# Last pass of a decode backward kernel: later use of the weight slabs in the background products, and an earlier start of the next group's dO product

## The chip, the cores and the metric

The kernel runs on one core of one Trainium2 chip. The metric is the device time of one execution in microseconds (us), taken as the median over several executions. Smaller is better.

## The reference

The program is forward and backward of four small layers applied to one token (batch 1, sequence 1, model width 1024): attention over a cache, a dense layer with squared ReLU, the same attention again, the same dense layer again. The attention has 32 query heads in four groups of eight; each group shares one key and one value cache of 65536 rows of 128 bf16 numbers (16 MB each). Weights are shared between the two uses.

```
x = x + A(layernorm(x))      # A: q = x wq; softmax(q k^T / sqrt(128)) v; times wo
x = x + B(layernorm(x))      # B: relu(x w1 + b1)^2 w2 + b2
x = x + A(layernorm(x))
x = x + B(layernorm(x))
out, vjp = jax.vjp(f, x, k_cache, v_cache, wq, wo, w1, b1, w2, b2)
return out, vjp(grad_out)    # the output and nine gradients
```

The large results are the gradients of the two caches (64 MB each), which are sums over both attention layers.

## The kernel before

The work is one token, so almost all of it is moving the caches through on-chip memory. Four passes go over them: pass 1 and pass 2 are the two attention forwards, pass 3 is the backward of the second attention, and pass 4 is the backward of the first attention, which also writes the gradients of both caches. Between the passes stand short dense stages for the feed-forward layers.

**Blocks and items.** A cache of one group is read in blocks of 32 x 128 rows, 1 MB each. An item is a quarter of a block (eight 128x128 tiles). A group has 64 items and pass 4 has 256 items, in the order `ITEMS[3]`, groups 3, 2, 1, 0. `pipeline` runs over the items; in round i it calls the stage functions with their lags: `vT` (TensorE transposes eight V tiles at L1249, and the result is copied to `kt`), `vS` two items later (scores at L1282, and at the end of a block the product X at L1290), `dV8` (gradient of V) three items later, and `k8` (dq at L1329 and the gradient of K) seven items later. The gradient blocks are built by `outer16` (matmuls at L1303, copies to the arena, one store of 1 MB by the POOL queue at L1309). After the stages of a round `bg.step(i)` advances the background work by at most one step.

**The arena.** All large buffers are granules of 1 MB in one tile called `arena`: 12 free ones and 8 that hold the softmax weights of both layers (one per layer and group) until pass 4 is done with a group. `Slot` takes a granule: loads of cache blocks (L331, by the SP queue), weight slabs (L425, also by SP) and store buffers all come from the same supply. A weight slab takes the granule that has been free longest. A granule that was stored from may be loaded again only when its store has landed.

**The background products.** Two of them use weights in pass 4. `g_dO` multiplies one group's share of `wo` with the gradient dx1 and gives dO, which a group needs before its first item (`bg.need(g)` in `vT` would run the rest of it at once). `g_dn` does the same with `wq` once a group's dq is complete, at round 70 for the first group. Both go through `g_rowdots`. It takes eight rows from two slabs of 1 MB (four rows each), first builds a broadcast vector `vbc` in `g_bcast_vec` (four steps), and then issues one multiplication on VectorE per row (L553, `mv_t`), whose sum ScalarE takes at L544. A slab is requested when its first row is asked for; the first four rows come from the first slab, and before row 4 the generator yields `"wait"` five times (`WAIT_STEPS`), one round each.

`Background` has a queue `urgent`, worked strictly first in, first out, a queue `normal` (the gradients of the weights, worked only in rounds in which the urgent work waits or is absent), and a list `later` of products that join `urgent` at a given round. `by_group` fills `later`: in pass 4 the dO of the second, third and fourth group join at rounds 32, 96 and 160.

**Who sets the order.** Passes 1 to 3 run inside `tc.manual_schedule`, so TensorE, VectorE and ScalarE execute in the written order. Pass 4 does not: there a planner at build time orders each engine's instructions. Among instructions that it holds to be ready it takes the one written first, and an instruction written later may go ahead of earlier ones while those wait. Each engine and each DMA queue then executes in that fixed order, with semaphore waits.

Of the kernel before, what the change touches and what calls it, by code (L numbers as in the profile page):

```python
# [20 lines left out]
def kernel(  # L21
# [46 lines left out]
    WAIT_STEPS = 5  # L68
# [13 lines left out]
    PS = {}  # L82
# [5 lines left out]
    def ps_tr(shape=None, dtype=BF):  # L88
        return PS["pool"].tile(shape or [P, 8, P], dtype, name="ps_tr", tag="tr", bufs=2 if PS["pass4"] else 3)
# [4 lines left out]
    def ps_gg():  # L94
        return PS["pool"].tile([P, 1024], F32, name="ps_gg", tag="gg", bufs=2)
# [4 lines left out]
    def ps_mv(shape, dtype=F32):  # L100
        if PS["pass4"]:
            return ps_tr(shape, dtype)
        return PS["pool"].tile(shape, dtype, name="ps_mv", tag="mv", bufs=1)
# [30 lines left out]
    def add_load(act=0.0, dve=0.0, pe=0.0):  # L134
        load["act"] += act
        load["dve"] += dve
        load["pe"] += pe
# [379 lines left out]
    def g_bcast_vec(vcol, nj):  # L517
        pt = ps_mv([nj, P], F32)
        nc.tensor.transpose(pt[:, :], vcol, ident_f[:, :])
        yield  # L520
        rows = tmp.tile([32, P], BF, name="bc_rows")
        nc.vector.tensor_copy(out=rows[0:nj, :], in_=pt[:, :])
        vbc = mvs.tile([P, nj * P], BF, name="vbc", tag="vbc", bufs=1)
        yield
        for j0 in range(0, nj, 4):
            pg = ps_gg() if PS["pass4"] else ps_tr([P, 512], F32)
            for jj in range(4):
                nc.tensor.matmul(pg[:, jj * P:(jj + 1) * P], lhsT=ident_b[0:nj, j0 + jj:j0 + jj + 1].to_broadcast([nj, P]),
                                 rhs=rows[0:nj, :], start=True, stop=True)
            nc.scalar.copy(out=vbc[:, j0 * P:(j0 + 4) * P], in_=pg[:, 0:512])  # L530
            add_load(act=0.6)
            yield
        return vbc

    def g_rowdots(slab_it, nk, vcol, nj, finish, name):
        n = nj * P
        y = vec.tile([P, nk], F32, name=name)
        nc.gpsimd.memset(y[:], 0.0)
        vbc = None
        due = None  # L540

        def total(t, kc):
            def f():
                nc.scalar.activation(out=t[:, :], in_=t[:, :], func=ACTF.Copy, accum_out=y[:, kc:kc + 1])  # L544
            return f
        for kc, slab in slab_it:
            if vbc is None:
                vbc = yield from g_bcast_vec(vcol, nj)
            elif kc % 4 == 0:
                for _ in range(WAIT_STEPS):  # L550
                    yield "wait"
            t = mvs.tile([P, n], BF, name="mv_t", tag="mv_t", bufs=2)
            nc.vector.tensor_tensor(out=t[:, :], in0=slab, in1=vbc[:, :], op=ALU.mult)  # L553
            add_load(dve=0.1 + n * 0.00054, act=0.42 + n * 0.00083)
            if due is not None:
                due()
            due = total(t, kc)
            yield
        due()
        yield  # L560
        r = finish(y[:, :])
        if r is not None:
            yield from r
        yield
# [167 lines left out]
    class Background:  # L732
# [35 lines left out]
        def by_group(self, p, gen):  # L768

            order = list(dict.fromkeys(g for g, _ in ITEMS[p]))  # L770
            n = len(ITEMS[p]) // G
            for k, g in enumerate(order[1:]):
                self.later.append((k * n + n // 2 if PS["pass4"] else k * n + n // 4, gen(g), g))

        def drain(self):
            while self.later:
# [115 lines left out]
    def g_dO(L, dx, g):  # L892
        yield from g_rowdots(wo_slabs(g)[0], R, dx[:], DC, dO_finish(L, g), "%s_dO%d" % (L["name"], g))
# [10 lines left out]
    def g_dn(L, dn, g, first):  # L904
        yield from g_rowdots(wq_slabs(g)[0], DC, L["dqT"][:, gsl(g)], R, dn_finish(dn, first), "%s_dn%d" % (L["name"], g))
# [770 lines left out]
```

## Time and profile before

| what | value |
|---|---|
| median of 8 runs | 2013.25 us |
| lowest and highest run | 2009.19 and 2017.61 us |
| profiled execution, its own time | 2017.61 us |
| its span in the trace | 2015.8 us |
| pass 4 in the trace, first and last X at L1290 | 1221.5 to 1980.8 us |
| read from and written to memory | 625 MB and 166 MB |
| mean rate over the span | 392 GB/s |
| PE, DVE, ACT, POOL busy | 81%, 58%, 52%, 7% of the span |

The profiled execution is the slowest of the eight, 4.4 us above the median. Its own time is 1.8 us more than its span. The first X and the last X lie 63 blocks apart, so a block of pass 4 takes 12.05 us on average and an item 3.0 us.

A row of the page's groups names the line, the engine, the operation and the tiles written and read, then the busy time and the mean duration, and after the bar the engine's idle time just before these instructions with what ended most of it. In the views by time the columns are start, duration, engine, line and operation, and in square brackets the idle time before.

### The profile page before, as it was taken

To read this page: it belongs to the slowest core of one execution; us is meant where nothing else is said; L and a number is where in the kernel's file an instruction comes from. 1 tells how busy PE (TensorE), PEld (TensorE's weight loads), DVE (VectorE), ACT (ScalarE), POOL (GpSimd) and SP (SyncE) were. 2 spreads that over 40 slices of the span, in tenths; PEclk is the share of its full clock that TensorE was granted. 3 is DMA by queue.
4 is the path that set the end of the run, shared out by engine and by line. 5 is a ranking of instruction groups with operands and counts; after the bars stand their busy time and mean duration, and the time that the engine had idled before them with its cause. 6 is when DMAs were issued, how large, how long until landed. Compare 5 with 4: busy or idle time off the path is not lost. (4 is left out here: it accounts for less than half of the span.)

```text
span 2015.8 us, 67001 instructions
## 1 busy us (share of the span) xinstructions
PE 1622.8 (81%) x30210; PEld 1317.9 (65%) x30210; DVE 1175.0 (58%) x2358; ACT 1043.9 (52%) x1613; POOL 144.4 (7%) x332
## 2 busy tenths in 40 slices
PE   6877788688877787878777888788788898698986
PEld 6877777687777786767677785455455455355554
DVE  5645455355545544535454466587668587578775
ACT  3444344253443353426353355586667587567665
POOL 0000000000000000000000001111111121111211
PEclk9989899698999997998998998799779699789888
DMA  9999999999999998999999986999999899899996
GB/s 389 421 419 420 419 423 402 392 399 419 420 418 421 419 400 313 365 419 420 420 417 413 391 304 262 356 407 424 420 417 421 343 422 422 355 423 425 423 369 242
DMA packets 110845, 794.97 MB, mean 394 GB/s; under 512 B 9424, under 2 KB 9438, under 8 KB 49374
## 3 DMA queue, kind: packets, MB, share of 16 engines
q1 hardware_dynamic: 86510, 624.99, 76.1%
q0 software_dynamic: 24048, 165.70, 19.9%
q8 instruction: 236, 3.87, 0.8%
q14 instruction: 51, 0.42, 0.1%
HBM read 624.96 MB, written 165.69 MB: 392 GB/s over the span
## 5 line engine op out<-in xcount | busy, mean ns | idle before, releaser
L153 DVE COPY kt<-ps_tr 128x1024 bf16<-128x1024 bf16 x724 | 497.4, 688 | 473.4 <-PE ps_tr L936 256.3
L150 ACT CAST arena<-ps_gg 128x1024 bf16<-128x1024 f32 x452 | 441.1, 1010 | 221.9 <-PE ps_gg L1303 173.5
L936 PE MATMUL ps_tr<-ident_b,arena 128*128 128x128 bf16 x3840 | 311.1, 226 | 62.1 <-DMA arena<-in_A_k_cache_dram 46.6
L936 PEld LDWEIGHTS <-arena 128*128 128x128 bf16 x3840 | 235.2, 101 | 69.1 <-DMA arena<-in_A_k_cache_dram 49.5
L153 DVE CAST arena<-ps_gg 128x1024 bf16<-128x1024 f32 (+1 forms) x191 | 228.8, 1198 | 82.6 <-PE ps_gg L1303 45.4
L150 ACT COPY kt<-ps_tr 128x1024 bf16<-128x1024 bf16 x164 | 171.2, 1049 | 184.6 <-PE ps_tr L1128 125.5
L1303 PE MATMUL ps_gg<-GG,xt 64*128 64x512 bf16 x1024 | 218.4, 424 | 49.4 <-DVE arena L153 28.4
L1038 PE MATMUL ps_acc<-arena 128*128 128x64 bf16 (+4 forms) x4096 | 205.8, 196 | 43.8 <-DMA arena<-in_A_v_cache_dram 25.8
L1249 PE MATMUL ps_tr<-ident_b,arena 128*128 128x128 bf16 x1824 | 179.6, 237 | 28.9 <-DMA arena<-in_A_v_cache_dram 28.1
L954 PE MATMUL ps_sc<-L_qpad,kt 128*128 128x64 bf16 (+7 forms) x3584 | 183.8, 194 | 17.5 <-issue 9.9
L1128 PE MATMUL ps_tr<-ident_b,arena 128*128 128x128 bf16 x1920 | 155.7, 227 | 51.6 <-DMA arena<-in_A_v_cache_dram 50.9
L1019 ACT ACTIVATE arena<-S_sb,L_negm 128x128 bf16<-128x128 f32 x256 | 165.6, 1003 | 56.7 <-DVE L_negm L1004 56.7
L1038 PEld LDWEIGHTS <-arena 128*128 128x128 bf16 x4096 | 159.9, 100 | 46.9 <-DMA arena<-in_A_v_cache_dram 29.8
L1249 PEld LDWEIGHTS <-arena 128*128 128x128 bf16 x1824 | 120.7, 105 | 86.7 <-issue 54.4
L954 PEld LDWEIGHTS <-kt 128*128 128x128 bf16 x3584 | 153.5, 100 | 22.2 <-issue 12.3
L1128 PEld LDWEIGHTS <-arena 128*128 128x128 bf16 x1920 | 117.7, 101 | 56.2 <-DMA arena<-in_A_v_cache_dram 53.8
L1329 PE MATMUL ps_acc<-X,arena 128*128 128x64 bf16 (+3 forms) x2048 | 120.4, 199 | 21.0 <-DMA arena<-in_A_k_cache_dram 21.0
L1019 ACT ACTIVATION_READ_ACCUMULATOR arena<-S_sb,L_negm 128x1 f32 x256 | 128.2, 501 | 0.0
L1329 PEld LDWEIGHTS <-arena 128*128 128x128 bf16 x2048 | 87.7, 102 | 56.1 <-issue 33.1
L1303 PEld LDWEIGHTS <-xt 64*128 64x128 bf16 x1024 | 61.1, 94 | 91.2 <-issue 54.2
L1282 PEld LDWEIGHTS <-kt 128*128 128x128 bf16 x1824 | 87.1, 104 | 50.1 <-issue 48.7
L1282 PE MATMUL ps_sc<-DOB,kt 128*128 128x64 bf16 (+3 forms) x1824 | 119.6, 202 | 0.0
(269 smaller groups left out, 2152.1 us busy)
## 6 DMA issues: line engine op xcount, KB each, us to landing
arena<-in_A_k_cache_dram SPq DMA_DIRECT2D x86, 2048.0 KB, 21.8
arena<-in_A_v_cache_dram SPq DMA_DIRECT2D x83, 2048.0 KB, 21.2
out_dram<-arena POOLq DMA_DIRECT2D x151, 1024.0 KB, 11.6
arena<-in_A_v_cache_dram SPq DMA_DIRECT2D x76, 1024.0 KB, 14.9
arena<-in_A_k_cache_dram SPq DMA_DIRECT2D x76, 1024.0 KB, 12.6
arena<-in_B_w_dram SPq DMA_DIRECT2D x32, 896.0 KB, 6.7
arena<-in_A_wq_dram SPq DMA_DIRECT2D x22, 1024.0 KB, 14.5
arena<-in_A_wo_dram SPq DMA_DIRECT2D x18, 1024.0 KB, 18.6
```

The lines of the kernel that those rows point to most:

```text
L150: nc.scalar.copy(out=out, in_=in_)
L153: nc.vector.tensor_copy(out=out, in_=in_)
L936: nc.tensor.transpose(pt[:, i, :], kb8[:, i, :], ident_b[:, :])
L954: nc.tensor.matmul(state["ps_s"][:, s:s + w, :].rearrange("p a b -> p (a b)"), lhsT=kt[:, i, :], rhs=L["qpad"][:, g, 0:w, :].rearrange("p ...
L1019: nc.scalar.activation(out=E(p, g, c0, SU)[:, :, h], in_=S[:, h, :], func=ACTF.Exp, bias=L["negm"][:, g, su, h:h + 1], scale=SCALE, accum_ ...
L1038: nc.tensor.matmul(ps_o[:, 0:w, :], lhsT=vb8[:, i, :], rhs=E(p, g, c, w), start=(c % SU == 0), stop=(c % SU == SU - 1), skip_group_check=True)
L1128: nc.tensor.transpose(pt[:, i, :], vb8[:, i, :], ident_b[:, :])
L1249: nc.tensor.transpose(pt[:, i, :], vb8[:, i, :], ident_b[:, :])
L1282: nc.tensor.matmul(state["ps_dp"][:, s:s + w, :].rearrange("p a b -> p (a b)"), lhsT=vt[:, i, :], rhs=DOB[:, g, 0:w, :].rearrange("p a b - ...
L1303: nc.tensor.matmul(pg[:, 512 * h:512 * h + 512], lhsT=xt[64 * h:64 * h + 64, j1 // 8 + m, :], rhs=gg[64 * h:64 * h + 64, :, :].rearrange(" ...
L1329: nc.tensor.matmul(ps_dq[:, 0:w, :].rearrange("p a b -> p (a b)"), lhsT=kb8[:, i, :], rhs=X[:, s:s + w, :].rearrange("p a b -> p (a b)"), ...
```

## The change

In `g_rowdots` the number of waiting steps is eight in pass 4 and five elsewhere. They stand before row 4 as before. New are waits after `g_bcast_vec`, before the first row: `steps - WAIT_STEPS + 1`, which is four in pass 4, and one in pass 3, which uses the same function. In `by_group` the second group's dO of pass 4 joins the urgent queue at round 16 instead of 32, the third group's at 72 instead of 96, and the fourth group's at 136 instead of 160.

```diff
@@ g_rowdots
         due = None
+        steps = 8 if PS["pass4"] else WAIT_STEPS
...
         for kc, slab in slab_it:
             if vbc is None:
                 vbc = yield from g_bcast_vec(vcol, nj)
+                for _ in range(steps - WAIT_STEPS + 1):
+                    yield "wait"
             elif kc % 4 == 0:
-                for _ in range(WAIT_STEPS):
+                for _ in range(steps):
                     yield "wait"
@@ by_group
             for k, g in enumerate(order[1:]):
-                self.later.append((k * n + n // 2 if PS["pass4"] else k * n + n // 4, gen(g), g))
+                self.later.append((k * n + 8 if PS["pass4"] and k else k * n + n // 4, gen(g), g))
```

Lines of the kernel named here and below are those before the change.

## The prediction

> **What bounds the kernel now.** I read the windows of 50 us over pass 4 first, then the waits of the dip, then the engine and queue timelines at it.
>
> ```profile
> core 0: us, PE busy (x) PEld busy (x) DVE busy (x) ACT busy (x) POOL busy (x), PEclk, DMA share, GB/s
> 1200.00:1250.00 50.00, 37.31 (x603) 26.88 (x604) 34.33 (x87) 26.33 (x31) 7.40 (x15) 0.90 0.69 264
> 1250.00:1300.00 50.00, 40.84 (x472) 24.50 (x471) 30.16 (x46) 28.14 (x31) 8.87 (x17) 0.76 0.92 345
> 1300.00:1350.00 50.00, 41.07 (x487) 25.36 (x487) 36.06 (x60) 38.14 (x51) 7.39 (x14) 0.86 1.00 402
> ...
> 1700.00:1750.00 50.00, 30.53 (x394) 19.66 (x392) 29.64 (x47) 28.61 (x39) 6.39 (x12) 0.80 0.90 361
> 1750.00:1800.00 50.00, 45.51 (x608) 28.38 (x604) 39.56 (x69) 35.87 (x39) 11.18 (x21) 0.97 1.01 416
> ```
>
> The last two columns carry it: from 1300 us on the 16 DMA engines are full, except in a few dips. The bound of pass 4 is the transfers, and a stall costs what it takes from them. The first 100 us are not full: there granules are missing. The dip at 1700 has one cause:
>
> ```profile
> DVE mv_t L553 <- DMA arena<-in_A_wo_dram: 16.3, 1, 16.3
> ```
>
> ```profile
> 1712.32 1.27 DVE L153 COPY kt<-ps_tr 128x1024 bf16<-128x1024 bf16 x2
> 1729.90 0.69 DVE L553 TENSOR_TENSOR mv_t<-arena,vbc 128x1024 bf16<-128x1024 bf16 x1 [16.30 <-DMA arena<-in_A_wo_dram]
> ```
>
> ```profile
> 1703.42 0.33 SPq L331 DMA_DIRECT2D arena<-in_A_v_cache_dram  x1
> 1707.43 3.63 SPq L331 DMA_DIRECT2D arena<-in_A_k_cache_dram  x2
> 1711.17 0.44 SPq L425 DMA_DIRECT2D arena<-in_A_wo_dram  x1
> ```
>
> VectorE stands for one slab (fourth group's dO, row 4), and every copy from PSUM behind it stands too. The slab was issued at 1711.17 and landed 18.6 us later; VectorE arrived 2.4 us after the issue. Of the 12 slabs in pass 4 used this way it is the only one waited for. Why was it issued late? In the built program its granule (a softmax plane) has long been free, but SP works in order, and the K load ahead waits for a store:
>
> ```profile
> SPq L331 <- DMA out_dram<-arena: 539.9, 94, 14.5
> SPq L425 <- DMA out_dram<-arena: 76.3, 13, 9.4
> ```
>
> That is how SP lives in this pass: stores land (median 11.7 us), then it issues.
>
> **What the Trainium skill says.** "Perfetto Trace Analysis", section "Sequencer Loop": an engine's instructions are queued and each waits for its semaphores. The trace agrees: the copies behind the row stood 16.3 us. "DMA: Bandwidth & Descriptors", section "Issuing engines are not separate DMA queues": transfers of all issuers share the same engines and interleave. It agrees: the loads of SP take 76.1% and the stores of POOL 19.9% of the same 16 engines. So a slab competes with both. The same page, section "Measured", gives 6.15 us for 1 MB alone; here slabs of pass 4 landed after 7.5 to 30.3 us, median 14.3, and I use these.
>
> **The change part by part.** No arithmetic and no byte is added or removed: 96 rows, the same loads, the same stores. What moves is order. I compared the built programs' order on each engine, placing each instruction by the item whose work stands before it, and each load by what holds it or its predecessors on SP.
>
> (a) Waits. Per product, four before row 0 and three more before row 4; six products, 42 rounds in pass 4. They cost no engine time: normal background work takes the rounds. g_dn grows from 19 to 26 rounds, g_dO from 21 to 28. Will a group be kept waiting? The second pair runs from 70 to 95 and 96 to 123, before the need at 128; the third ends at 187, before 192. Cost 0. If they overran, the remaining rows would come at once, some 3 us.
>
> (b) The joining round. The queue is first in, first out, and g_dn joins at 70. So the dO that joins at 72 begins at 96, as before; the last at 160, as before. Only the second group's dO really moves, from 32 to 16. Cost of the rest 0.
>
> (c) Is the slab used eight items after its request? No: the planner pulls it forward. The stalled row was written at item 173.6 and stands after the copy of item 169.0; in the changed program it is written at 180.7 and stands after 174. The store that holds SP ahead of it moves too, from the one of item 162.6 to 166.6. Distance 6.4 items before, 7.4 after: one item gained, at about 2.5 us unstalled. **The wait does not go, it shrinks to about 13 us** (bounds 8 and 16). A saving in the end time is smaller: the dip took 10% of 50 us from the DMA engines, 5.0 us for 16.3 us of stall. So -1 us (bounds 0 and -3).
>
> (d) The second group's dO, at 16. Its second slab (row 4) now stands on SP behind a K load that waits for the scores of item 29, and the row stands on VectorE after the copy of item 29.8. Distance 0.7 items; before, the same slab had 7 to 8. So VectorE arrives 2 to 3 us after the issue, and loads land there in 7.5 to 11.1 us (K, V and slab loads of 1240 to 1320). **A new wait of 5 to 9 us**, with all copies behind it. DMA share there is 0.92, so the cover is thinner than at 1700: end time between a third of it and all, +2 to +9, taken +5.
>
> (e) Its first slab takes a granule that a K load had, when only 12 circulate. The K load for item 19 moves from behind the scores of item 13 to behind a store, and seven loads between items 19 and 40 have only 5 to 6.5 items from release to use (a store counted as five items), against three before. K and V waits of 1240 to 1320 are 17 us now. I take +2 us (bounds 0 and +8). On the other side, 1 MB leaves the full stretch at 1311 for a less full one, 1 MB at 421 GB/s: -1.5 us (bounds -2.5 and 0).
>
> (f) Third group's dO: its first slab gets 5.6 items, 17 us at 3.0 us, against a landing of 14 to 18.6. +0.5 us (0 to +3).
>
> (g) Pass 3: one wait in each of six products; no row waits there for a slab. SP moves a slab by one or two places. 0 (bounds -1 and +2).
>
> POOL's stores keep their number and nearly their order; some move past a neighbour, priced in the bounds of (e). Sum: -1 + 5 + 2 - 1.5 + 0.5 = +5. The profiled execution took 2017.61 us for a span of 2015.8, the slowest run shown; against it the changed kernel would take 2022.6, against the median of 2013.25 it is **2018 us**. Its own range, the bounds not all at one end: 2014 to 2026.
>
> **The rivals.**
>
> *Faster: the wait goes.* If the transfers ahead of the slab are lighter at 174 than they were, the row finds it landed, and (d) hides in the slack of the unfilled start. For it: landings range from 7.5 to 30.3 us, and the wait decides at a landing of about 5 us after issue, or at 6 items more of distance. Against it: SP's order shows 1 more item, and the three loads just ahead are still there. Gain: 5 us by DMA share, up to 12 if later blocks don't give it back. After the stall the trace gives back part already: the four blocks behind it took about 10 us against a mean of 12. So 2001 to 2008, say 2006.
>
> *No change.* The transfers bound the pass and a ring of granules absorbs what VectorE does: stalls only move. For it: share 1.00 to 1.02 in most windows. 2010 to 2016, about 2013.
>
> *Much slower: the start breaks.* With two slab granules out of 12 between items 13 and 40, each K load behind the SP queue comes late, and each late one delays the store that the next waits for. It decides when three or more of the seven tight loads each stall 4 to 8 us; with (d), 2026 to 2038.
>
> *The change doesn't do what it says* is in the forecast: (b) and (c).
>
> **How the numbers follow.** A difference under 0.2% (4 us) cannot be told from none. Forecast 45% (slower by more 36, same 9); start breaks 12% (slower); no change 21% (same 18, faster 2, slower 1); faster rival 22% (faster 20, same 2). Together faster 0.22, same 0.29, slower 0.49. The range reaches from inside the faster case to inside the broken start, 2004 to 2034.
>
> **What would show it.** Right: a wait of mv_t for in_A_wo in two places, one near item 30 (about 1285 us) and one near item 174 (about 1745), together 16 to 25 us; DMA share under 0.95 in a window at both; dO of the third group still beginning near item 96. Wrong: no wait of mv_t over 3 us (faster rival), or none near item 30 and the time unmoved (no change), or K and V waits of 1240 to 1320 at twice the 17 us (broken start).

## The result, and the profile after

The changed kernel takes **2024.63 us** (median of 11 runs, 2020.39 to 2031.16), the kernel before 2011.45 us beside it (median of 32). The ratio is 1.0062, with an interval of [1.0051, 1.0073]. The forecast was slower, by 5 us; it was slower by 12.5 us by the ratio (0.0062 of 2012; 13.2 us between the two medians). The profiled execution took 2023.42 us for a span of 2021.6 us. That is only 5.8 us more than the span of before, whose profiled execution was the slowest of those first shown. So the two traces show where the change acts, and the sizes must come from the runs.

In the lines below line numbers are higher than before from line 541 on, by 1 at L545 and by 3 from L556 on: `mv_t` is L556, X is L1293. `xin` (L1256 before, L1259 now) is a copy on POOL of the softmax weights of the next block.

The windows of 50 us over pass 4 first, with the same columns as those of before:

```profile
core 0: us, PE busy (x) PEld busy (x) DVE busy (x) ACT busy (x) POOL busy (x), PEclk, DMA share, GB/s
1200.00:1250.00 50.00, 36.03 (x606) 25.89 (x602) 34.56 (x84) 26.43 (x30) 7.12 (x14) 0.95 0.69 261
1250.00:1300.00 50.00, 39.26 (x459) 23.90 (x457) 32.23 (x44) 31.27 (x39) 7.82 (x16) 0.78 0.96 376
...
1500.00:1550.00 50.00, 34.20 (x421) 22.08 (x421) 31.52 (x57) 29.44 (x41) 6.52 (x12) 0.78 0.83 322
...
1700.00:1750.00 50.00, 30.96 (x309) 19.00 (x308) 21.81 (x34) 21.87 (x27) 5.24 (x10) 0.63 1.01 404
```

The window where the forecast put a new cost, 1250 to 1300, is fuller than before (0.96 against 0.92). The dip is at 1500 to 1550, where before had 1.01. Before had a dip of its own one window later, 0.90 at 1550 to 1600, which is 1.01 now; taken together, the two windows moved 1.15 MB less than before (745 against 768 GB/s in sum), which is about 3 us of transfers. At 1700 to 1750 the DMA engines are now full, but the compute engines still stand, with TensorE at 309 matmuls against 394. VectorE waited for weight slabs in pass 4 as follows (engine, tile and line, what ended the wait, total us, times, longest):

```profile
DVE X L1293 <- DMA arena<-in_A_wo_dram: 30.1, 2, 19.5
DVE mv_t L556 <- DMA arena<-in_A_wo_dram: 1.7, 1, 1.7
```

This is the odd line of the case. `mv_t` reads the slabs of `wo` and hardly waits. **X waits for them, 30.1 us in two places, and X reads no weight**: it multiplies scores with softmax weights. VectorE's timeline at the first and at the second:

```profile
1491.50 0.69 DVE L153 COPY kt<-ps_tr 128x1024 bf16<-128x1024 bf16 x1 [0.17 <-PE ps_tr L1252]
1511.67 0.69 DVE L1293 TENSOR_TENSOR X<-ps_sc,arena 128x512 bf16<-128x512 f32 x1 [19.48 <-DMA arena<-in_A_wo_dram]
```

```profile
1733.16 1.21 DVE L153 CAST arena<-ps_gg 128x1024 bf16<-128x1024 f32 x1
1744.97 0.69 DVE L1293 TENSOR_TENSOR X<-ps_sc,arena 128x512 bf16<-128x512 f32 x1 [10.59 <-DMA arena<-in_A_wo_dram]
```

And the loads on SP, from two stretches of its timeline, and `xin` on POOL ahead of the second slab:

```profile
1478.21 7.32 SPq L331 DMA_DIRECT2D arena<-in_A_v_cache_dram  x2
1485.62 0.65 SPq L331 DMA_DIRECT2D arena<-in_A_k_cache_dram  x1
1486.38 0.89 SPq L425 DMA_DIRECT2D arena<-in_A_wo_dram  x1
...
1728.37 0.56 SPq L425 DMA_DIRECT2D arena<-in_A_wo_dram  x1
```

```profile
1727.72 0.62 POOL L1259 COPY xin<-arena 128x512 bf16<-128x512 bf16 x1
```

The first slab was issued at 1486.38 and landed 25.2 us later, the second at 1728.37 and landed after 16.5 us. Both times VectorE was free for X about 6 us after the issue (1492.19 and 1734.37) and X stood until the landing. The second is the slab for which `mv_t` stood 16.3 us before the change. It went out 0.03 us after this `xin` had ended (1728.34).

What stood behind the first of them, in the timelines of TensorE and of POOL:

```profile
1512.42 0.61 PE L1265 MATMUL ps_tr<-ident_b,X 128*128 128x128 bf16 x4 [19.65 <-DVE X L1293]
```

```profile
1514.71 0.30 POOL L1232 CAST CC<-cf 128x128 bf16<-128x128 f32 x1 [22.23 <-PE ps_tr L1234]
```

TensorE's transposes of X and POOL's queue, which also issues the stores, waited as long. POOL issued no store between 1491.94 and 1518.36 us, and SP no load between 1502.87 and 1522.59. The transfers ran down only after the stall, as windows of 10 us show:

```profile
1500.00:1510.00 10.00, 0.00 (x0) 0.00 (x0) 0.00 (x0) 0.00 (x0) 0.00 (x0) 0.50 1.02 416
1510.00:1520.00 10.00, 7.58 (x66) 5.14 (x66) 4.46 (x8) 2.91 (x4) 2.10 (x4) 0.50 0.63 260
1520.00:1530.00 10.00, 8.85 (x117) 5.47 (x116) 8.53 (x15) 8.47 (x13) 1.15 (x2) 0.92 0.74 288
```

While every engine stood, loads and stores issued earlier kept the DMA engines full; then 6.3 us of their time were lost in 20 us. At the second stall SP issued two more loads (1740.41 and 1743.62), and the share fell only to 0.91 in the 10 us behind it.

**Why X waits.** X and `xin` take the softmax weights of both layers through one view, `E2(g)`: granule 12+g for one layer and 16+g for the other. In the built programs the semaphores are set as if such an access touched everything from 12+g to 16+g. A group that is done frees its two softmax granules, and a slab takes the oldest free granule. If it is one that lies between, it is bound on both sides to instructions that don't touch it. (An item number in the table says behind which item's work the instruction is written: X of item 165 belongs to the block of items 160 to 163.)

| slab, built program | granule | its load waits for | and then who waits for it |
|---|---|---|---|
| before: fourth dO's second, asked for in round 168 | 14 | X of item 165, xin of 167 | `mv_t`, one place ahead of X on VectorE, and xin of 171 |
| after: third dO's first, round 96 | 15 | X of item 93, xin of 95 | X of item 97, xin of 99 |
| after: fourth dO's second, round 172 | 14 | X of item 169, xin of 171 | X of item 173, xin of 175 |

So such a slab can't go out before the X or xin just ahead, and the next X can't run before it has landed. Whether the row is used five or eight items after the request doesn't matter: the X in between waits in any case. Before had one such slab, after has two, because other holding times and other rounds make another granule the oldest in round 96. I call this the **false operand**.

### The profile page after: what moved, and what is told of

It is laid out like the page before. It is cut to its first block, busy times and chain, and to the rows that moved or that the text cites. A ratio compares the mean times of both kernels' runs of the same rounds, so it can differ in the third digit from the quotient of the medians.

```text
span 2021.6 us, 67004 instructions
## 1 busy us (share of the span) xinstructions
PE 1617.3 (80%) x30210; PEld 1320.4 (65%) x30210; DVE 1173.5 (58%) x2361; ACT 1042.2 (52%) x1610; POOL 143.4 (7%) x332
## 5 line engine op out<-in xcount | busy, mean ns | idle before, releaser
L150 ACT CAST arena<-ps_gg 128x1024 bf16<-128x1024 f32 (+1 forms) x455 | 442.9, 1012 | 248.3 <-PE ps_gg L1306 193.7
L153 DVE CAST arena<-ps_gg 128x1024 bf16<-128x1024 f32 (+1 forms) x188 | 224.5, 1194 | 86.2 <-PE ps_gg L1306 40.9
L1306 PE MATMUL ps_gg<-GG,xt 64*128 64x512 bf16 x1024 | 214.1, 416 | 39.3 <-ACT arena L150 19.6
L1252 PE MATMUL ps_tr<-ident_b,arena 128*128 128x128 bf16 x1824 | 176.6, 235 | 30.3 <-DMA arena<-in_A_v_cache_dram 29.0
L957 PE MATMUL ps_sc<-L_qpad,kt 128*128 128x64 bf16 (+7 forms) x3584 | 183.8, 194 | 20.1 <-issue 13.2
L957 PEld LDWEIGHTS <-kt 128*128 128x128 bf16 x3584 | 153.5, 100 | 26.7 <-issue 16.9
L1176 PE MATMUL ps_acc<-dsT,arena 128*128 128x64 bf16 (+7 forms) x2048 | 105.5, 197 | 14.4 <-DMA arena<-in_A_k_cache_dram 11.6
L1285 PE MATMUL ps_sc<-DOB,kt 128*128 128x64 bf16 (+3 forms) x1824 | 114.5, 201 | 0.0
## 6 DMA issues: line engine op xcount, KB each, us to landing
arena<-in_A_k_cache_dram SPq DMA_DIRECT2D x76, 1024.0 KB, 12.5
```

Of the source, the lines that this page charges most:

```text
L150: nc.scalar.copy(out=out, in_=in_)
L153: nc.vector.tensor_copy(out=out, in_=in_)
L957: nc.tensor.matmul(state["ps_s"][:, s:s + w, :].rearrange("p a b -> p (a b)"), lhsT=kt[:, i, :], rhs=L["qpad"][:, g, 0:w, :].rearrange("p ...
L1176: nc.tensor.matmul(ps_dq[:, 0:w, :].rearrange("p a b -> p (a b)"), lhsT=kb8[:, i, :], rhs=dsT[:, s:s + w, :].rearrange("p a b -> p (a b)") ...
L1252: nc.tensor.transpose(pt[:, i, :], vb8[:, i, :], ident_b[:, :])
L1285: nc.tensor.matmul(state["ps_dp"][:, s:s + w, :].rearrange("p a b -> p (a b)"), lhsT=vt[:, i, :], rhs=DOB[:, g, 0:w, :].rearrange("p a b - ...
```

## The experiments

There are two ways to take the false operand away without touching a wait or a round. All ratios are against the kernel before, with 95% intervals.

**1. Slabs kept out of the softmax granules** (`after_low`: the changed kernel; `before_low`: the kernel before).

```diff
-        by_age = sorted((t, i) for i, t in FREE.items())
+        by_age = sorted((t, i) for i, t in FREE.items() if not low or i < NSLOT)
...
-                sl = Slot(name)
+                sl = Slot(name, low=PS["pass4"])
```

> The changed kernel, except that in pass 4 a weight slab takes only granules of the ring's first twelve, never a freed softmax plane. Theory of the false operand: X (the block product on VectorE) waited 30.1 us for in_A_wo although it reads no weight, because it reads the softmax weights of both layers through one access pattern over granules 12+g to 16+g, and a slab put between them is taken for its operand. Then here X waits less than 3 us for in_A_wo; the dip of 1500 to 1550 (DMA share 0.83, so 8.5 us of transfers lost) goes; time 8 to 13 us under the changed kernel: 0 to +5 us against the kernel before. Rival, held granules: the longer wait holds slabs' granules longer and K and V loads come late; then the X wait may go but the time stays at +10 to +13 us, or worse, since slabs now come out of the same twelve granules (+15 to +20). Rival, the early dO: the second group's dO at item 16 costs at the start; then +8 or more stays too, with X times behind by that much from block 10 on.

Measured: 2012.57 us, 0.9999 [0.9987, 1.0011]. X waits no more for `in_A_wo`; `mv_t` does for 3.7 us, near 1288 us. The windows at the two places:

```profile
1500.00:1550.00 50.00, 42.70 (x557) 27.15 (x556) 40.02 (x73) 39.30 (x52) 8.47 (x15) 0.93 1.00 406
...
1700.00:1750.00 50.00, 33.91 (x366) 20.79 (x364) 27.45 (x44) 26.95 (x34) 6.10 (x11) 0.73 0.96 368
```

The dip at 1500 is gone (share 1.00 against 0.83, 557 matmuls against 421). At 1700 TensorE does more than in the changed kernel (366 against 309), though less than in the one before, and the share is 0.96. With its slabs kept low the changed kernel is level with the kernel before: 0.0063 of the time goes.

> The kernel before with slabs of pass 4 kept to the first twelve granules. It has one slab between the planes that X reads (fourth group's dO, row 4), and mv_t stands 16.3 us for it just ahead of an X that would stand for it too. False operand: the slab's place alone doesn't move mv_t, which reads it in truth, so mv_t may still wait for it, 5 to 16 us, and the time is within -5 to +2 us of before. Held granules: fewer granules for K and V, +3 to +10 us.

Measured: 2007.33 us, 0.9970 [0.9960, 0.9981]. No row waits for a slab at all, so the expectation that `mv_t`'s wait might stay was wrong, and the gain, 6.0 us, is just past the 5 us that were expected at most. Experiment 2 shows that this wait too came from the false operand.

**2. The reads split by layer** (`after_split`, `before_split`): the granules stay as they are.

```diff
-                nc.gpsimd.tensor_copy(out=split2(xin[:, :, :]), in_=E2(g, c8, J))
+                for l in range(2):
+                    nc.gpsimd.tensor_copy(out=split2(xin[:, :, :])[:, :, l, :], in_=E(l, g, c8, J))
...
-                nc.vector.tensor_tensor(out=split2(X[:, :, :]), in0=split2(ps_dp[:, :, :]), in1=E2(g, c0, J), op=ALU.mult)
+                for l in range(2):
+                    nc.vector.tensor_tensor(out=split2(X[:, :, :])[:, :, l, :], in0=split2(ps_dp[:, :, :])[:, :, l, :],
+                                            in1=E(l, g, c0, J), op=ALU.mult)
```

> The changed kernel with the granules as they are, but the two reads of the softmax weights (VectorE's X product and GpSimd's xin copy) are each split into one instruction per layer, so that none spans the granules between. This adds 64 instructions on VectorE and 64 on GpSimd, X of 128x256 in place of 128x512; VectorE is busy 0.73 of the time, so some 0.2 us more for each pair is at most 13 us of busy time, most of it beside other work. False operand: no wait of X for in_A_wo, time 5 to 13 us under the changed kernel (0 to +8 against before). Held granules or early dO: the X wait goes and the time stays at +10 to +16.

Measured: 2011.28 us, 0.9993 [0.9982, 1.0003]; no wait of X for a slab, one of `mv_t` of 4.6 us. The loss goes here too, with the slabs in granules 15 and 14 as in the changed kernel. So it is the operand and not which granules the slabs take. In the planned order the slabs also moved: these two go out at 1408.42 and 1598.73 us, where they went out at 1486.38 and 1728.37.

> The kernel before with the reads of the softmax weights split by layer, granules and waits as they are. mv_t waited 16.3 us there for a slab that it does read, one place ahead of X on VectorE. If the slab was late for mv_t in its own right: mv_t still waits 8 to 16 us and the time is within 3 us of before. If a planner's or SP's order follows from the false operand (the slab is asked for earlier once X doesn't bind it): the wait goes and the time is 3 to 7 us under before, as with low slabs.

Measured: 2010.24 us, 0.9988 [0.9977, 0.9999]. The wait of 16.3 us is gone, though neither the slab's granule nor its use was moved. SP's timeline shows why; these are the two slabs of the fourth group's dO with the reads split:

```profile
1591.06 0.38 SPq L425 DMA_DIRECT2D arena<-in_A_wo_dram  x1
1595.78 0.56 SPq L425 DMA_DIRECT2D arena<-in_A_wo_dram  x1
```

The second goes out at 1595.78. In the kernel before it went out at 1711.17, 115 us later. In the built program its load now waits for a transfer of item 127 alone, and the planner puts it that early. In the kernel before it was held back behind X of item 165 and xin of item 167, which is this one:

```profile
1707.78 0.61 POOL L1256 COPY xin<-arena 128x512 bf16<-128x512 bf16 x1 [2.21 <-PE ps_tr L1262]
```

It ended at 1708.39, so of the 115 us the store that SP waited for can have cost at most the last 2.8. The time follows in part: the gain is 0.0012, by its interval between 0.0001 and 0.0023, where 3 to 7 us were expected and low slabs gained 0.0030.

The two cures don't reach equally far. Store buffers lie between the softmax granules as well, and in the built programs X and xin are tied in the same way to the copies into them. Low slabs leave that as it is. The traces of `after_low` (first line) and of `waits_low` (second) show such waits:

```profile
DVE X L1293 <- ACT arena L150: 2.8, 2, 1.9
```

```profile
POOL xin L1259 <- ACT arena L150: 17.9, 2, 17.1
```

In the three kernels with split reads neither X nor xin has such a wait. What these waits cost wasn't measured; near the one of 17.1 us TensorE also stood 9.5 us for a block of V. So "low slabs" takes the false operand away from the slabs only.

**3. The change's two halves, with the false operand and without.** `waits_only` and `waits_low` have the change's waits and the old joining rounds, `join_only` and `join_low` (and `join_split`) the new joining rounds and the old waits.

```diff
# waits_only: the changed kernel, but
-                self.later.append((k * n + 8 if PS["pass4"] and k else k * n + n // 4, gen(g), g))
+                self.later.append((k * n + n // 2 if PS["pass4"] else k * n + n // 4, gen(g), g))
# join_only: the kernel before, but
-                self.later.append((k * n + n // 2 if PS["pass4"] else k * n + n // 4, gen(g), g))
+                self.later.append((k * n + 8 if PS["pass4"] and k else k * n + n // 4, gen(g), g))
```

> The change's waits alone: eight items of waiting per slab in pass 4 and one more in pass 3, the dO products begin where they did in the kernel before. By its order the fourth dO's second slab lies between the planes that X reads and is asked for at round 172, X of round 173 behind it; none of the third dO's slabs does. False operand: one X wait of 8 to 18 us near item 173 in place of mv_t's 16.3, none near 1500 us; time -3 to +4 us against before. Held granules: the longer waits are all of the change's +13, so +8 to +13 here. Early dO: -3 to +4 here as well, so this run alone doesn't tell it from the false operand; the two runs of the changed kernel do.

> The change's waits alone (dO products begin where they did before), slabs of pass 4 kept to the first twelve granules. Without the false operand the change still costs 0.0029 of the time (changed kernel with low slabs 0.9999, kernel before with low slabs 0.997), some 6 us, and this run says which half of it does. If the early dO costs it (theory): like the kernel before with low slabs, -4 to -8 us against before, no wait of mv_t or X for in_A_wo over 3 us. If the longer waits cost it (rival, held granules): -2 to +3 us.

> The change's joining rounds alone, with the short waits of the kernel before and slabs in any granule. By its built order slabs asked for at rounds 89 and 153 lie between the planes that X and xin read, so both stand behind them two to four rounds later, and the dO rows stand behind their own. False operand: two waits for in_A_wo on VectorE or GpSimd of 5 to 20 us each near items 91 and 155, none near 173; time +4 to +16 us against before. If the false operand matters only with the long waits: within 3 us of before.

> The change's joining rounds alone (dO of the second group at item 16, of the others eight items into a group; short waits as before), slabs kept to the first twelve granules. Early dO (theory): it carries the 6 us that the change costs without the false operand, so -2 to +3 us against before, with a wait of mv_t near 1285 us. Held granules (rival): -4 to -8 us, as the kernel before with low slabs.

> The change's joining rounds with the short waits, the reads of the softmax weights split by layer, slabs in any granule. Against joining rounds alone (1.0018, 28.5 us of X waits for in_A_wo) it takes away the false operand and leaves the granules. False operand: no such wait, 0.994 to 0.998. If low slabs helped by how the ring is shared and not by the operand: 1.000 to 1.003.

Measured, with the wait of VectorE that low slabs take away, from one profiled execution each (`mv_t`'s in the first row, X's in the others):

| waits, joining rounds | slabs anywhere | wait, us | low slabs | reads split |
|---|---|---|---|---|
| old, old (before) | 1 | 16.3 | 0.9970 [0.9960, 0.9981] | 0.9988 [0.9977, 0.9999] |
| new, old | 1.0019 [1.0010, 1.0028] | 12.4 | 0.9995 [0.9986, 1.0004] | not run |
| old, new | 1.0018 [1.0007, 1.0030] | 28.5 | 0.9954 [0.9938, 0.9971] | 0.9971 [0.9960, 0.9982] |
| new, new (after) | 1.0062 [1.0051, 1.0073] | 30.1 | 0.9999 [0.9987, 1.0011] | 0.9993 [0.9982, 1.0003] |

The waits behind the second column, of `join_only` and of `waits_only`:

```profile
DVE X L1290 <- DMA arena<-in_A_wo_dram: 28.5, 2, 16.2
```

```profile
DVE X L1293 <- DMA arena<-in_A_wo_dram: 12.4, 1, 12.4
```

`waits_only` has the one X wait in place of `mv_t`'s, as the false operand said, and none near 1500. `join_only`, 3.6 us slower, came out just under the 4 to 16 us that were expected; its two waits are about where they were expected. POOL's xin stood at the same two places, 35.1 us for `in_A_wo`, and at another 9.9 us for `in_A_wq`; the column doesn't count these. By columns: low slabs take off 0.0030, 0.0024, 0.0064 and 0.0063, that is 6.0, 4.8, 12.9 and 12.7 us for waits of 16.3, 12.4, 28.5 and 30.1 us. If all of it is put down to VectorE's wait, **a stall here costs about 0.4 of its length** (0.37 to 0.45; with the intervals of the ratios 0.2 to 0.6). That is an estimate: the cure moves other things too. With the reads split the three rows give 0.0012, 0.0047 and 0.0069 (0.15 to 0.46), with added instructions in them.

By rows, the new joining rounds alone do no harm: -0.0016 with low slabs, -0.0017 with split reads, in both with intervals that overlap or touch those of the old rounds; with the long waits it is +0.0004 (low slabs). The theory that the early dO costs, on which the expectations of `waits_low` and `join_low` rested, has fallen; `join_low` gained 9.3 us, more than either theory had said. The new waits cost +0.0025 (low, old rounds), +0.0045 (low, new rounds), +0.0022 (split, new rounds).

**4. Why the waits cost.** The waits make a slab hold its granule longer, and pass 3 has one wait more. `ahead_low` is `waits_low` with the added waits of pass 4 ahead of the request, `waits4_low` is `waits_low` without the wait of pass 3, and `short_join_low` is `join_low` with three rounds in place of five.

```diff
# ahead_low, in g_rowdots
+            if p4 and seen in (0, 4):
+                for _ in range(4 if seen == 0 else steps - WAIT_STEPS):
+                    yield "wait"
+            nxt = next(it, None)
...
# waits4_low, after g_bcast_vec
-                for _ in range(steps - WAIT_STEPS + 1):
+                for _ in range(4 if PS["pass4"] else 0):
# short_join_low, before row 4
-                for _ in range(WAIT_STEPS):
+                for _ in range(3 if PS["pass4"] else WAIT_STEPS):
```

> As the change's waits alone with low slabs, and as many rounds per product, but the added waits of pass 4 stand ahead of a slab's request and not behind it: a slab is used 4 to 5 rounds after its request, as in the kernel before, and holds its granule no longer. Longer waits with low slabs stood at 0.9995 where short ones stood at 0.997. If the holding of granules costs that (theory): here 0.996 to 0.998, -4 to -8 us against before. If the later rounds of the products, or the wait added in pass 3, cost it (rival): 0.9985 to 1.0005, -3 to +1 us.

> The change's waits with low slabs, but without the one wait per product that it adds in pass 3. Long waits with low slabs stood at 0.9995, short ones at 0.997, and with the waits put ahead of the request at 0.9984, between the two. If pass 3's wait carries the rest: 0.9965 to 0.998, and the first X of pass 4 earlier by 2 us or more. If pass 3's wait costs nothing, as forecast: 0.9985 to 1.0005, the first X of pass 4 within 4 us of before's 1221.5.

> The change's joining rounds with low slabs (0.9954), and the wait ahead of a product's second slab cut from five rounds to three in pass 4. If each round that a slab holds a granule costs: 0.1 to 0.2% less again, 0.9935 to 0.995. If the short wait makes rows arrive ahead of their slab: waits of mv_t for in_A_wo or in_A_wq over 4 us and 0.996 or more.

Measured: `ahead_low` 0.9984 [0.9974, 0.9994], `waits4_low` 1.0004 [0.9993, 1.0014], `short_join_low` 0.9977 [0.9968, 0.9985]. Pass 3's wait costs nothing: without it the time is no lower, and the first X of pass 4 comes 0.1 us before that of before. `ahead_low` lies between 0.9970 and 0.9995, and its interval overlaps both. `short_join_low` holds its slabs for less time and is slower than `join_low` (the two intervals just overlap), with no wait of `mv_t` over 2.6 us. So holding is at most a part of it, and how the longer waits cost their 0.2 to 0.45% **stays open**.

**The lowest time** is that of `join_low`: 2004.38 us in six runs, 0.9954 of the kernel before, so 0.9893 of the changed one by the two ratios (0.9954 / 1.0062). Its interval overlaps or touches those of `before_low` and `join_split` (0.9971), so it isn't shown to be better than these.

## Why the prediction was right, and where its steps failed

The direction was right and the time, 12.5 us more where 5 was said, lay in the range. Much of that was luck: the term that carried the forecast, (d), hardly came, and the loss came from terms that stood at 0 and +0.5. A DMA share under 0.95 in a window at both places, which was to show that the forecast was right, came at neither (0.96 and 1.01). The working was right in few of its places: "a wait of mv_t for in_A_wo in two places, together 16 to 25 us" became 1.7 us of `mv_t` and 30.1 us of X.

- **What bounds the pass**: held. The dip, the stall and the late slab are one thing, and stalls cost less than their length. Its rate, 5.0 us of DMA time for 16.3 us of stall (0.31), lies within what the runs allow.
- **Why the slab was late**: wrong, and this is the step that failed. "In the built program its granule has long been free, but SP works in order, and the K load ahead waits for a store." The store was there, but it was the smaller part. The granule is free in the kernel's own account, yet the slab's load carries semaphores of X of item 165 and xin of 167, and that xin ended 2.8 us before the slab went out. With the reads split it went out 115 us earlier.
- **(a)** Waits at no cost: wrong, by +0.0022 to +0.0045 where no slab is a false operand. No overrun explains it: after the change the rows of the third group's dO run one by one, the last at 1541.82 us. The working looked at engine time; what it left out isn't settled.
- **(b)** First in, first out: in agreement. After the change the vector for the third group's dO is begun (`bc_rows`) at 1491.05 us, between X of item 93 and X of item 97.
- **(c)** "The wait does not go, it shrinks to about 13 us": the size was near (10.6 us), the owner wrong. It stood on X, and by the built order no distance of the row could have moved it.
- **(d)** A new wait of 5 to 9 us near item 30, +5: mis-sized. It was 1.7 us, and 3.7 and 4.6 us in the two cured kernels. The wait ended 9.6 us after the slab's issue at 1278.58, which fits the landings of the forecast (7.5 to 11.1), but VectorE came for it 7.9 us after the issue, and not 2 to 3. Together with **(e)** it was to cost 5.5 us; the joining rounds alone, no slab a false operand, came out 0.0016 to 0.0017 lower, some 3 us, and in no case 5.5 us higher.
- **(e)** TensorE's waits for K and V of 1240 to 1320 were 13.9 us (17.3 before), so the start does not break.
- **(f)** Third group's dO, +0.5 (0 to +3): the term that was mis-sized most. Its first slab landed after 25.2 us and not 14 to 18.6, and made X, which the term didn't look at, stand 19.5 us: some 8 us by the estimate of 0.4, some 6 us by the DMA time lost in the two windows of 10 us behind it.
- **(g)** Pass 3 at 0: nothing speaks against it; without its wait (`waits4_low`) the time is no lower.

The sum by the runs: low slabs take 0.0063 off the changed kernel and 0.0030 off the one before, so the slabs as false operands make +0.0033 of the difference; the rest, 0.9999 against 0.9970, is +0.0029; together 0.0062. With split reads the shares are +0.0057 and +0.0005. The middle values put more than half of the loss on the false operand in either case. But each ratio is uncertain by about 0.001, so with low slabs its share may also lie under half; the border between the parts depends on the cure and isn't fixed better than that.

On the rivals: *the wait goes* did come true for `mv_t`, and the time got worse all the same, since the next instruction on VectorE took the wait over. *No change* is excluded by the interval, and *the start breaks* by (e).

"Perfetto Trace Analysis", section "Sequencer Loop", says that an instruction stands until its semaphores allow it, and the trace agrees in a way that the prediction missed: the semaphores are those that were built in, and not those that the data needs. VectorE stood 19.5 us for a transfer of which X reads nothing.

## What to carry to other kernels

When a wait names a tile, ask whether the waiting instruction reads it. If not, look for an access pattern whose two ends enclose that tile's memory: split the access, or keep other data out of the gap. Before a wait is covered by distance, find out in the built program what holds the transfer back: if it is tied to a neighbour on both sides, distance gives nothing, and the wait only changes its name.

## What the runs showed that was not expected

Stops of VectorE of 12 to 30 us in all cost by the estimate only about 0.4 of their length in this pass, and the trace shows why: for most of the stop of 19.5 us the transfers issued before it went on at a share of 1.02, and only the 20 us behind it were thin. And the slab that mattered needed 25.2 us from issue to landing, where the slabs in pass 4 of the kernel before took 7.5 to 30.3 us, with a median of 14.3.
